# Second pair's gate and up blocks: the fifth K chunk's high-by-low products in seven-product form

## Chip, cores and metric

One core of a Trainium2 chip runs the whole kernel. The metric is device time in microseconds of one launch, the median over runs.

## The reference

```python
def _A_ref(x, wqkv, wo):                     # linear attention, 32 heads of 20
    ...
    pq, pk = phi(q), phi(k)                  # phi(t) = where(t > 0, t + 1, exp(t)) + 1e-6
    kv = jnp.einsum("bhsd,bhse->bhde", pk, v)
    ...
    return (lambda x, *d: x.transpose(*d))(o, 0, 2, 1, 3).reshape(B, S, D) @ wo

def _B_ref(x, w_gate, w_up, w_down):
    g = jnp.einsum("bsd,df->bsf", x, w_gate)
    u = jnp.einsum("bsd,df->bsf", x, w_up)
    h = _sigmoid(g) * u
    return jnp.einsum("bsf,fd->bsd", h, w_down)

g = _sigmoid((x * gate_w).sum(-1, keepdims=True))
return g * a + (1 - g) * b                   # S 2048, D 640, F 1536, all float32
```

The change concerns `x @ w_gate` and `x @ w_up` for the second half of the work.

## The kernel before

TensorE reads each float32 number as two parts, a high one (the rounded value) and a low one (the rest). A product of 128x128 weights with 128x512 of x is three matmuls in `mm3` (lines 406 to 408): high by high, high by low, low by high. `split` makes the parts: a copy on ScalarE (line 419), a difference on VectorE (line 423). `vec3` (line 427) is VectorE's (a op scalar) op b.

x has 2048 columns, in four groups of 512. The groups go in pairs, groups 2 and 3 first (`pr` = 1), then 0 and 1 (`pr` = 0, called the second pair here). K = 640 is five chunks of 128. On a pair (two column groups) and on gate and up (two weight matrices) the first four chunks are multiplied in a form with fewer products: sums of weights and sums of x, seven products of halves in place of eight. The fifth chunk is left over and multiplied plainly.

`f_phase(pr, ...)` runs F = 1536 as twelve blocks f = 0 to 11. A block (`Block`, steps `s1` to `s7`) has 18 products, so 54 matmuls, into running sums in PSUM: `ch` (s1, s3, s5, s6), `dd` (s2) and `cc` (s4, s7). ScalarE copies `ch` out between the steps, and `dd` starts from a copy of `ch` ("seed"). The weights of a block come in three forms: `W[n, 0]` the gate (tile `wg`, 640 KB), `W[n, 1]` (`wu`, 384 KB), and `W[n, 2]` the sums, nine chunks of 128 columns in two parts (`ws`, 1152 KB). The first pair makes them and stores them in DRAM; the second loads them with `load_form` through SP. `wg` and `wu` have two buffers; `ws_tile` takes turns between two. x stands in SBUF in `xf`: plain parts `a` and `b` of the two groups, and sums `t`.

The order in `f_phase` is f: s3, s4, s5; then f+1: s1; f: s6; f+1: s2; f: s7. In odd blocks from 3 on, the four parts d0 to d3 of a down pair (`down_pair`, 18 products of h with w_down) lie in between: d0 behind s3, d1 behind s4, d2 behind s5, d3 behind s1 of the next. Their weights come as one tile `wf`, loaded with `load_wf` behind s7 of the odd block before.

Which VectorE and ScalarE work goes where is settled when the program is made: the class `Order` keeps a model of the engines' times and puts pieces of work from queues between the steps (`fill`, `_stream` by due time, `need` when a step cannot go without). Among this work in the second pair are the denominators of the attention (`queue_dens`, on the tile `fac`: VectorE writes its groups from loads `pden`, stores them to `den_dram`, and reads back factors, `fac<-fac_dram`, through SP), the forms of the mixing matrix M (`queue_m`, tiles `mr` and `mt`), and the scaling and splitting of groups for the last stage. In that stage M's chunks `MHL[k, part]` (ten of 640 columns), loaded with `load_m`, are multiplied with `pq`, on top of seeds made on VectorE from `bl` and `omg`.

DMAs are issued on two queues, SP's and GpSimd's (POOL), each in order (line 363). An issue waits on its queue for what the load overwrites.

The lines of the loads of the second pair before:

```python
            if f + 2 < FC and not pr:
                for i in {2: (0,), 6: (1,), 7: (2,)}.get(s, ()):
                    load_form(("f", 0, f + 2), i)
```

Of the kernel before, what the change touches and what calls it, by code (L numbers as in the profile page):

```python
# [14 lines left out]
P = 128  # L15
# [15 lines left out]
class Order:  # L31

    def __init__(self):
        self.slack(False)
        self.pe = self.act = self.vec = 0.0
        self.items, self.lazy, self.chain, self.spare, self.soon, self.urgent = [], [], [], [], [], []
        self.kept = []
        self.made, self.used, self.done, self.before, self.tags, self.seeded = {}, {}, {}, {}, {}, {}
        self.streams, self.plan, self.base, self.turn = {}, {}, 0.0, 0
        self.busy = False  # L40
        self.parts = self.pend = None

    def slack(self, long):
# [216 lines left out]
    def mm(self, out, w, first, *aps):  # L260
        at = self.data(out if first else None, aps)
        if not first:
            p = self.place(out)
            at = max(at, self.last(self.used, p), self.seeded.get(p[0], 0.0))
        self.pe = max(self.pe, at)
        self.pe += 0.014 + w / 2400
        for ap in (*aps, out):
            self.busy_till(self.place(ap)[0], [self.pe + P_LAG])

    def when(self, ap):  # L270
        return self.last(self.made, self.place(ap))
# [98 lines left out]
def v_cost(w):  # L370
    return 0.07 + w / 960

@with_exitstack
def gated_mix_kernel(ctx: ExitStack, tc: tile.TileContext, x0, xt, xn, wk, wv, wo, wst_q, wst_f, out_t):
# [10 lines left out]
    def f32(ap):  # L385
        return ap.bitcast(F32)

    def width(ap):
        n = 1
        for s in ap.shape[1:]:  # L390
            n *= s
        return n
# [17 lines left out]
        order.mm(out, width(out), False, l_hi, r_lo)  # L410
        order.mm(out, width(out), False, l_lo, r_hi)

    def prod(out, terms, first):
        for n, t in enumerate(terms):
            mm3(out, *t, first and n == 0, n == len(terms) - 1)

    def act(out, src, fn, after="", **kw):
        order.on_act(width(out), after, out, src)
# [39 lines left out]
    fac = common.tile([P, NG, TG], F32, name="fac")  # L458
# [881 lines left out]
    class Block:  # L1340
# [53 lines left out]
        def s7(self):  # L1394
            prod(self.cc, [self.xb(2, 2 + j, 2 + j) for j in range(2)] + [self.xb(2, 4, 4)], False)
            add(self.c12, self.cc, self.c12, "p")

    spare_e = []

    def phi_q(g, u, src, after="p"):  # L1400
# [51 lines left out]

    def queue_dens(*gs2):

        st = {}

        def load(g, u):
            if u < KC:
                st[g, u] = tt("pden")
                gp.dma_start(st[g, u], p_dram[:, u, g])  # L1460
                st["at", g, u] = lambda: order.when(st[g, u])

        def one(g, u):
            td = fac[:, g]
            if u == 0:
                vec1(td, st[g, u], zcol[:, 0:1], zeps[:, 0:1], OP.mult, OP.add)
            else:
                vec3(td, st[g, u], zcol[:, u:u + 1], td, OP.mult, OP.add)
            load(g, u + 2)
            if u == KC - 1:  # L1470
                gp.dma_start(den_dram[:, g], td)
                st["at", g, u + 1] = lambda: order.when(den_dram[:, g])

        def turn_in(g):
            for j in range(4):
                js = slice(j * H, (j + 1) * H)
                gp.dma_start(fac[js, g].rearrange("h (d c) -> h d c", c=P),
                                  den_dram[:, g, j * P:(j + 1) * P].rearrange("(d h) c -> h d c", h=H))
            st[g, "gs"] = tt("gs")[:, :P]
            sp.dma_start(st[g, "gs"], gate_rep[4 * g:4 * g + 4].rearrange("i h c -> (i h) c"))  # L1480
            st["at", g, KC + 1] = lambda: max(order.when(fac[:, g]), order.when(st[g, "gs"]))

        def factor(g):
            td = fac[:, g]
            q = td[:, :P]
            add(td[:, :2 * P], td[:, :2 * P], td[:, 2 * P:])
            add(q, q, td[:, P:2 * P])
            order.on_vec(5 * P, "")
            nc.vector.reciprocal(q, q)
            vec2(q, q, st[g, "gs"], OP.mult)  # L1490
            gp.dma_start(fac_dram[:, g], q)
            st["at", g, KC + 2] = lambda: order.when(fac_dram[:, g])

        def turn_out(g):
            for d in range(4):
                sp.dma_start(fac[d * H:(d + 1) * H, g].rearrange("h (j c) -> h j c", c=P),
                                  fac_dram[:, g].rearrange("(j h) c -> h j c", h=H))
        order.add(0, 0, lambda: [load(g, u) for u in range(2) for g in gs2], chain=True)
        for u in range(KC):
            for g in gs2:  # L1500
                order.add(0, v_cost(TG), lambda g=g, u=u: one(g, u), None, lambda g=g, u=u: st["at", g, u]() + DEN_LAG, chain=True)
        for n, (v, fn) in enumerate(((0, turn_in), (2.0, factor), (0, turn_out))):
            for g in gs2:
                order.add(0, v, lambda g=g, fn=fn: fn(g), ("fac", g) if n == 2 else None,
                          lambda g=g, n=n: st["at", g, KC + n](), chain=True)
# [186 lines left out]
    WF = 2 * D + 8 * P  # L1692
    wf = []

    def load_wf(p):

        t = wf_tile()
        wf[:] = [t]
        for c0, c1 in ((D, 2 * D), (0, D), (2 * D, WF)):
            sp.dma_start(f32(t[:, :, c0:c1]), wd_dram[p][:, :, c0:c1])  # L1700

    def wf_tile():
        return down_pool[1].tile([P, 2, WF], F32R, name="wf", tag="wf")
# [480 lines left out]
    def q_phase(pr, b12, extra):  # L2184
# [8 lines left out]
        for j, (u, b) in enumerate(steps):  # L2193
            if isinstance(u, Block):
# [25 lines left out]
                if pr:  # L2220
                    if blk is A and s == 2:
                        queue_g(B.n)
                        queue_s(B.n, 0, 1)
                        queue_both(nx, 3)
                        queue_s(B.n, 1)
                    elif blk is A and s == 3:
                        queue_g(("f", pr, 0))
                    elif blk is A and s == 6:
                        load_w()
                    elif blk is A and s == 7:  # L2230
                        queue_s(("f", pr, 0))
                else:
                    n = {2: ((B, "f", 0, 0), (B, "f", 1, 0)), 6: ((A, "f", 0, 1), (B, "f", 1, 1)),
                         7: ((A, "f", 0, 2), (B, "f", 1, 2))}
# [27 lines left out]
    def f_phase(pr, q, hooks={}):  # L2262
# [14 lines left out]
        def step(f, s):  # L2277
            order.at((pr, f, s))
            n = ("f", pr, f)
            if s == 1:  # L2280
                order.need(("wg", n))
                blocks[f] = Block(n, f > 1 or f and not pr)
            else:
                order.need((nx[1], s))
            if pr and s == 7 and f + 1 < FC:
# [10 lines left out]
            if s == 3 and f == 0 and not pr:  # L2296
                for _ in q:
                    pass
                after_f(f, blk, 2)
# [30 lines left out]
        for f in range(FC):  # L2330
# [3 lines left out]
            if f in dens[pr]:  # L2334
                queue_dens(*dens[pr][f])
            if f % 2 and f > 1:
                if pr:
                    pass
                elif f == FC - 1:
                    while any(it[3] == "m" for it in order.spare) or order.pend:  # L2340
                        order.need("m")
                        order._flush()
                    load_m(0)
                down = down_pair(pr, f // 2 - 1)
            for s in (3, 4, 5):
                step(f, s)
# [127 lines left out]

    def load_m(i):

        n = (0, 3, 10)
        t = (ws_tile, wf_tile)[i]().rearrange("p a b -> p (a b)")[:, :(n[i + 1] - n[i]) * D]
        sp.dma_start(f32(t), mp_dram.rearrange("p a b c -> p (a b c)")[:, n[i] * D:n[i + 1] * D])
# [181 lines left out]
    class ABlock(Block):  # L2661
# [118 lines left out]
    pq_tiles(2)  # L2780
    queue_pq(2)
    load_p(3)
    pq_tiles(3)
    queue_scale(3)
    queue_pq(3)
# [109 lines left out]
```

## Time and profile before

| | us |
|---|---|
| median of three runs | 725.4 (724.84 to 725.54) |
| span of the profiled execution | 723.4 |
| TensorE busy | 719.2 (3412 matmuls) |
| VectorE busy | 580.2 |
| ScalarE busy | 365.7 |
| first matmul of s3 of f=1 in the second pair | at 451.06 |
| last block's s7 ends | at 643.57 |

The profile is of one execution, and its span runs from the first instruction to the last; the time of a run has what lies around the span as well, and the profiled execution's own time is not given apart from its span. Times of rows are from the span's start. In rows of instructions the engine follows start and duration; "PE" is TensorE's matmul, "PEld" its weight load, "DVE" VectorE, "ACT" ScalarE, "SPq" the SP queue. Matmuls overlap, so a record of one is longer than the distance to the next. Helpers record the operations, so many rows share a line; the tile names tell them apart.

### The profile page before, as it was taken

How to read it: one execution, taken by the hardware profiler on the slowest of the kernel's cores; microseconds unless marked ns; L12 is line 12 of the kernel's file. 1: busy time of each engine (PE TensorE's matmuls, PEld its weight loads, DVE VectorE, ACT ScalarE, POOL GpSimd, SP SyncE). 2: the span in 40 equal slices, each digit the busy share in tenths (PEclk: the TensorE clock that was granted, in tenths of full speed). 3: DMA queues.
4: the chain of work that ended last, by engine and by line, in shares of the span. 5: the costliest groups of instructions: out<-in, count | busy, mean ns of one | idle time of the engine just before them, and what ended most of it. 6: DMA issues, size and time to landing. Idle time of an engine off the chain costs nothing.

```text
span 723.4 us, 9843 instructions
## 1 busy us (share of the span) xinstructions
PE 719.2 (99%) x3412; PEld 608.4 (84%) x3412; DVE 580.2 (80%) x1008; ACT 365.7 (51%) x682; POOL 117.9 (16%) x199
## 2 busy tenths in 40 slices
PE   9999999999999999999999999999999999999998
PEld 8999999888888888888888888888888888888887
DVE  4988878987687889898988886467666878589995
ACT  5764748267656653545455862454334242325551
POOL 0311111113311211111211133013001213000100
PEclk9999999999999999999999999999999999999999
DMA  8464658698787866457688778976959595868733
GB/s 280 115 199 114 185 129 266 139 325 291 285 316 257 325 236 240 171 216 262 241 330 322 212 253 344 394 242 213 359 169 392 177 400 158 310 258 310 195 59 131
DMA packets 65129, 177.59 MB, mean 246 GB/s; under 512 B 11723, under 2 KB 25179, under 8 KB 61495
## 3 DMA queue, kind: packets, MB, share of 16 engines
q1 hardware_dynamic: 45126, 104.03, 43.0%
q0 software_dynamic: 19664, 72.70, 29.1%
q8 instruction: 27, 0.44, 0.3%
q10 hardware_dynamic: 288, 0.23, 0.1%
q14 instruction: 24, 0.19, 0.1%
HBM read 104.62 MB, written 67.33 MB: 238 GB/s over the span
## 4 chain that ended last, share of the span: by engine, by line
PE 99%; DVE 0%; ACT 0%; issue 0%
PE ch L406 11%; PE ch L408 11%; PE ch L407 11%; PE cc L406 9%; PE cc L408 9%; PE cc L407 9%; PE dd L406 7%; PE dd L408 7%; PE dd L407 7%; PE rot L408 6%; PE rot L406 6%; PE rot L407 6%; PE rot L1577 1%; PE rot L511 0%; PE ch L996 0%; PE dd L996 0%
## 5 line engine op out<-in xcount | busy, mean ns | idle before, releaser
L423 DVE TENSOR_TENSOR hf<-c,hf 128x512 fp32r<-128x512 f32 x77 | 52.5, 687 | 19.5 <-ACT hf L419 19.1
L419 ACT ACTIVATE hf<-c 128x512 fp32r<-128x512 f32 (+1 forms) x79 | 48.5, 625 | 36.8 <-DVE c L423 36.8
L419 ACT ACTIVATE c<-ch 128x512 f32<-128x512 f32 x43 | 25.7, 598 | 73.4 <-PE ch L408 67.7
L423 DVE TENSOR_TENSOR c<-cc,c 128x512 f32<-128x512 f32 x38 | 26.2, 689 | 28.2 <-PE cc L408 15.9
L406 PE MATMUL ch<-xth,ws 128*128 128x512 f32 x112 | 43.8, 391 | 0.0
L408 PE MATMUL ch<-xth,ws 128*128 128x512 f32 x112 | 43.6, 390 | 0.0
L407 PE MATMUL ch<-xtl,ws 128*128 128x512 f32 x112 | 43.6, 389 | 0.0
L423 DVE TENSOR_TENSOR tb<-rot,tb 128x512 f32<-128x512 f32 x60 | 39.1, 684 | 2.6 <-PE rot L408 2.6
L423 DVE TENSOR_TENSOR tb<-dd,tb 128x512 f32<-128x512 f32 x41 | 28.2, 688 | 11.3 <-PE dd L408 11.2
L423 DVE TENSOR_TENSOR c<-c,c 128x512 f32<-128x512 f32 x48 | 33.0, 687 | 2.6 <-ACT c L419 2.0
L419 ACT ACTIVATE c<-dd 128x512 f32<-128x512 f32 x21 | 12.6, 598 | 43.4 <-PE dd L408 43.4
L406 PE MATMUL dd<-xrh,wg 128*128 128x512 f32 x84 | 32.9, 392 | 0.0
L408 PE MATMUL dd<-xrh,wg 128*128 128x512 f32 x84 | 32.7, 389 | 0.0
L407 PE MATMUL dd<-xrl,wg 128*128 128x512 f32 x84 | 32.7, 389 | 0.0
L406 PE MATMUL cc<-xbh,ws 128*128 128x512 f32 x84 | 32.7, 389 | 0.0
L407 PE MATMUL cc<-xbl,ws 128*128 128x512 f32 x84 | 32.7, 389 | 0.0
L408 PE MATMUL cc<-xbh,ws 128*128 128x512 f32 x84 | 32.7, 389 | 0.0
L419 ACT ACTIVATE dd<-ch 128x512 f32<-128x512 f32 x22 | 12.8, 583 | 32.2 <-PE ch L408 32.2
L423 DVE TENSOR_TENSOR wst<-wst 128x256 f32<-128x256 f32 (+2 forms) x69 | 27.4, 412 | 1.4
L408 PEld LDWEIGHTS ch<-xth,ws 128*128 128x128 f32 x112 | 21.0, 188 | 4.7 <-DVE ws L423 0.3
L407 PEld LDWEIGHTS ch<-xtl,ws 128*128 128x128 f32 x112 | 21.0, 188 | 4.3
L406 PEld LDWEIGHTS ch<-xth,ws 128*128 128x128 f32 x112 | 21.0, 188 | 4.1
(710 smaller groups left out, 2347.4 us busy)
## 6 DMA issues: line engine op xcount, KB each, us to landing
wf<-ws POOLq DMA_DIRECT2D x12, 1152.0 KB, 7.6
ws<-wf SPq DMA_DIRECT2D x11, 1152.0 KB, 9.6
wst<-wst_f SPq DMA_DIRECT2D x12, 640.0 KB, 5.0
wf<-wg POOLq DMA_DIRECT2D x12, 640.0 KB, 6.8
wd<-wd POOLq DMA_DIRECT2D x12, 640.0 KB, 8.2
wg<-wf SPq DMA_DIRECT2D x12, 640.0 KB, 6.9
wf<-wd SPq DMA_DIRECT2D x10, 640.0 KB, 11.0
xnst<-xn SPq DMA_DIRECT2D x16, 320.0 KB, 3.8
```

Source lines behind the costliest of these rows:

```text
L406: nc.tensor.matmul(out, l_hi, r_hi, start=first, stop=False, skip_group_check=True)
L407: nc.tensor.matmul(out, l_hi, r_lo, start=False, stop=False, skip_group_check=True)
L408: nc.tensor.matmul(out, l_lo, r_hi, start=False, stop=last, skip_group_check=True)
L419: nc.scalar.activation(out, src, fn, **kw)
L423: nc.vector.tensor_tensor(out, a, b, op=op)
L1577: nc.tensor.matmul(ps[:w, :w], v[:, m, :w], gt[:, m, c0:c0 + w], start=(m == 0), stop=(m == KC - 1))
```

## The change

In blocks f = 1 to 11 of the second pair the fifth chunk, too, is done with shared products, but only its high-by-low and low-by-high parts: the three high-by-high products stay, and sums of low parts (with the factor `UP`, 4096, to keep parts apart) are put in places where the sums of the first four chunks already run. `EBlock` has 53 matmuls in place of 54. It needs four sums of x (`ET`, made once, at f = 0) and three 128x128 sums of weights per block (`queue_e`). The tiles for these come out of the space of the sums' second buffer: one `ws` tile holds the `ET` and the chunk "d" of two blocks, the other the pieces of the sums of one block (`EF["w"]`), so that each piece is loaded when its step in the block before is through; f = 1 takes its pieces in `fac`. The loads of `wf` and of M move.

```diff
+    def prod(out, terms, first, singles=()):
+        ...
+        for n, (w, x) in enumerate(singles):
+            nc.tensor.matmul(out, w, x, start=False, stop=n == len(singles) - 1, skip_group_check=True)
...
+    def e_pieces(f):
+        base = EF["f" if f == 1 else "w"]
+        for i, (c0, n) in enumerate(((0, 4), (4, 4), (8, 8))):
+            EW[f, i] = base[:, c0 * P:(c0 + n) * P].rearrange("p (a c) -> p a c", a=2)
+        e = EF["x"]
+        EW[f, "d"] = e[:, 12 * P:14 * P] if f % 2 else e[:, 16 * P:]
+        EW[f, "u"] = e[:, 14 * P:16 * P] if f % 2 else EF["w"][:, 16 * P:]
+
+    def load_piece(f, i):
+        src = w_dram["f", f, 2]
+        if i == "d":
+            sp.dma_start(f32(EW[f, i]).rearrange("p (a c) -> p a c", a=2), src[:, :, 4 * P:5 * P])
+        else:
+            c0, n = ((0, 2), (2, 2), (5, 4))[i]
+            sp.dma_start(f32(EW[f, i]), src[:, :, c0 * P:(c0 + n) * P])
+
+    def queue_e(f):
+        ...
+            vec3(u[:, :P], f32(dh), -1 / UP, f32(ul), OP.mult, OP.add)
+            vec3(u[:, P:], f32(ul), UP, f32(uh), OP.mult, OP.add)
+            vec3(dl, f32(dh), 1 / UP, f32(dl), OP.mult, OP.add)
+        order.add(0, 3 * v_cost(P), fn, ("e", f), lambda: max(order.when(d), order.when(WT[n, 1])),
+                  stream=("e", f), due=order.due((0, f, 3)))
+
+    def queue_et(late):
+        (ah, al), (bh, bl) = xf.a(4, every), xf.b(4, every)
+        if late:
+            def t3():
+                vec3(bl, f32(bh), 1 / UP, f32(bl), OP.mult, OP.subtract)
+        ...
+        for k, fn in ((2, lambda: sub(t[0], f32(bl), f32(al))),
+                      (2, lambda: vec3(t[1], f32(t[0]), -UP, f32(bh), OP.mult, OP.add)),
+                      (4, lambda: sub(t[2], f32(ah), f32(t[1])))):
+            order.add(0, v_cost(TG), fn, ("et", k), stream=("et", 0), due=order.due((0, 1, 3)))
+
+    class EBlock(Block):
+        ...
+        def s1(self):
+            self.ch, self.dd = ps_tile("ch"), ps_tile(self.tag)
+            gh, _, _, xl = self.xa(0, 4, 4)
+            prod(self.ch, [self.xa(0, j, j) for j in range(2)], True, [(gh, xl)])
+            act(self.dd, self.ch, AF.Copy, "p")
+        def s2(self):
+            gh, gl, xh, _ = self.xa(0, 4, 4)
+            prod(self.dd, [self.xa(0, k, k) for k in range(2, 4)], False, [(gh, xh), (gl, xh)])
+        def s3(self):
+            order.need(("et", 2), False)
+            order.need(("e", f), False)
+            prod(self.ch, self.xt(2, 0, 1), False, [(self.e("u")[0], ET[2])])
+        def s4(self):
+            prod(self.cc, self.xt(2, 7, 0), True, [(uh, xh), (self.e("u")[1], ET[1])])
+        def s5(self):
+            prod(self.ch, self.xt(2, 5, 2), False, [(self.e("d")[0], ET[3])])
+        def s6(self):
+            prod(self.ch, self.xt(1, 0, 3), False, [(uh, xh), (ul, ET[4])])
+        def s7(self):
+            prod(self.cc, [self.xb(2, 2 + j, 2 + j) for j in range(2)], False, [(w, xh) for w in self.e("d")])
...
+        nonlocal fac                       # in queue_dens
+        if "f" in EF:
+            EF.pop("f")
+            fac = fac_tile()
...
+                    if s == 7 and blk is B:            # in q_phase, ahead of f = 0
+                        EF["x"] = order.in_views(ws_tile().rearrange("p a b -> p (a b)"))
+                        EF["f"] = order.in_views(fac_tile(F32R).rearrange("p a b -> p (a b)"))
+                        e_pieces(1)
+                        for i in (0, 2, 1, "d"):
+                            load_piece(1, i)
...
+            if 1 < f < FC - 1 and not pr and s in (3, 5, 7):
+                load_piece(f + 1, {3: 0, 5: 2, 7: 1}[s])
+            if f and not f % 2 and s == 5 and not pr:
+                load_wf(f // 2 - 1, True)              # the last cut of wf
             if f + 2 < FC and not pr:
-                for i in {2: (0,), 6: (1,), 7: (2,)}.get(s, ()):
+                for i in {2 if f < 2 else 3: (0,), 6: (1,)}.get(s if f < 2 or s != 6 else 0, ()):
                     load_form(("f", 0, f + 2), i)
+                if s == 7 and f == 0:
+                    queue_et(True)
+                    EF["w"] = order.in_views(ws_tile().rearrange("p a b -> p (a b)"))
+                    e_pieces(2)
+                    for i in ("d", 0, 2, 1):
+                        load_piece(2, i)
+                    queue_e(2)
+                elif s == 7:
+                    e_pieces(f + 2)
+                    load_piece(f + 2, "d")
+                    if f > 1:
+                        load_form(("f", 0, f + 2), 1)
+                    queue_e(f + 2)
...
             for _ in down:
                 pass
+            if not pr and f % 2 and f > 1:
+                load_wf(f // 2) if f < FC - 1 else load_m(0)
...
-            if not pr and f % 2 and 1 < f < FC - 1:    # was behind step(f, 7)
-                load_wf(f // 2)
...
-        n = (0, 3, 10)                                 # load_m: chunks 0 to 2 in ws, 3 to 9 in wf
-        t = (ws_tile, wf_tile)[i]().rearrange("p a b -> p (a b)")[:, :(n[i + 1] - n[i]) * D]
+        n = (0, 7, 10)                                 # chunks 0 to 6 in wf, 7 to 9 in ws
+        t = (wf_tile, ws_tile)[i]().rearrange("p a b -> p (a b)")[:, :(n[i + 1] - n[i]) * D]
...
-        (FC - 1, 7): [lambda: load_m(1)],
...
     load_p(3)
+    load_m(1)
```

`load_m(0)` stood ahead of s3 of f = 11 before, and moves behind its down pair. `in_views` and `views` make `Order` keep account of a tile by its parts.

More of the change, by code (lines that the diff above doesn't have):

```diff
@@ L267, in mm, with in_views @@
         for ap in (*aps, out):
-            self.busy_till(self.place(ap)[0], [self.pe + P_LAG])
+            p = self.place(ap)
+            self.busy_till(p[0], [self.pe + P_LAG])
+            if p[0] in self.views:
+                self.note(self.used, p, [self.pe + P_LAG])
+    def in_views(self, ap):
+        name = self.place(ap)[0]
+        self.before[name] = None
+        self.views.add(name)
+        return ap
     def when(self, ap):
@@ L411, in mm3 @@
         order.mm(out, width(out), False, l_lo, r_hi)
-    def prod(out, terms, first):
+    def prod(out, terms, first, singles=()):
         for n, t in enumerate(terms):
-            mm3(out, *t, first and n == 0, n == len(terms) - 1)
+            mm3(out, *t, first and n == 0, n == len(terms) - 1 and not singles)
+        for n, (w, x) in enumerate(singles):
+            nc.tensor.matmul(out, w, x, start=False, stop=n == len(singles) - 1, skip_group_check=True)
+            order.mm(out, width(out), False, w, x)
     def act(out, src, fn, after="", **kw):
@@ L457, in gated_mix_kernel, with fac_tile @@
     common.tile([P, 8], F32, name="shift")
-    fac = common.tile([P, NG, TG], F32, name="fac")
+    def fac_tile(dt=F32):
+        return common.tile([P, NG, TG], dt, name="fac", tag="fac")
+    fac = fac_tile()
     p_dram = dram.tile([P, KC, NG, TG], F32, name="p_dram")
@@ new lines, in queue_e, with fn @@
+    def queue_e(f):
+        n = ("f", 0, f)
+        d, u = EW[f, "d"], EW[f, "u"]
+        dh, dl = d[:, :P], d[:, P:]
+        uh, ul = (W[n, 1][c][:, 2 * P:] for c in range(2))
+        def fn():
+            vec3(u[:, :P], f32(dh), -1 / UP, f32(ul), OP.mult, OP.add)
[3 more added lines that the diff above has]
+                  stream=("e", f), due=order.due((0, f, 3)))
@@ new lines, in queue_et @@
+    def queue_et(late):
[3 more added lines that the diff above has]
+                vec3(bl, f32(bh), 1 / UP, f32(bl), OP.mult, OP.subtract)
+            order.add(0, v_cost(TG), t3, ("et", 3), stream=("et", 3), due=order.due((0, 1, 5)))
+            ET[3] = bl
+            return
+        t = [EF["x"][:, i * TG:(i + 1) * TG] for i in range(3)]
+        ET.update({1: t[0], 2: t[1], 4: t[2]})
+        for k, fn in ((2, lambda: sub(t[0], f32(bl), f32(al))),
+                      (2, lambda: vec3(t[1], f32(t[0]), -UP, f32(bh), OP.mult, OP.add)),
+                      (4, lambda: sub(t[2], f32(ah), f32(t[1])))):
+            order.add(0, v_cost(TG), fn, ("et", k), stream=("et", 0), due=order.due((0, 1, 3)))
@@ new lines, in gated_mix_kernel, with w, e @@
+    class EBlock(Block):
+        def w(self, i, c):
+            if i < 2:
+                return super().w(i, c)
+            f = self.n[2]
+            i, c = (0, c) if c < 2 else (1, c - 2) if c < 4 else (2, c - 5)
+            t = EW[f, i][:, :, c * P:(c + 1) * P]
+            return t[:, 0], t[:, 1]
+        def e(self, k):
+            t = EW[self.n[2], k]
+            return t[:, :P], t[:, P:]
+        def s1(self):
[6 more added lines that the diff above has]
+            prod(self.dd, [self.xa(0, k, k) for k in range(2, 4)], False, [(gh, xh), (gl, xh)])
+            self.c11 = c_tile("c11")
+        def s3(self):
+            f = self.n[2]
+            order.need(("et", 2), False)
+            order.need(("e", f), False)
+            self.c12 = c_tile("c12")
+            prod(self.ch, self.xt(2, 0, 1), False, [(self.e("u")[0], ET[2])])
+            act(self.c12, self.ch, AF.Copy, "p")
+        def s4(self):
+            self.cc = ps_tile("cc")
+            uh, _, xh, _ = self.xb(1, 2, 4)
+            prod(self.cc, self.xt(2, 7, 0), True, [(uh, xh), (self.e("u")[1], ET[1])])
+        def s5(self):
+            order.need(("et", 3), False)
+            self.c22 = c_tile("c22")
+            prod(self.ch, self.xt(2, 5, 2), False, [(self.e("d")[0], ET[3])])
+            act(self.c22, self.ch, AF.Copy, "p")
+            add(self.c22, self.cc, self.c22, "a")
+        def s6(self):
+            order.need(("et", 4), False)
+            uh, ul, xh, _ = self.xa(1, 2, 4)
+            prod(self.ch, self.xt(1, 0, 3), False, [(uh, xh), (ul, ET[4])])
+        def s7(self):
+            xh = xf.b(4, every)[0]
+            prod(self.cc, [self.xb(2, 2 + j, 2 + j) for j in range(2)], False, [(w, xh) for w in self.e("d")])
+            add(self.c12, self.cc, self.c12, "p")
@@ L1453, in queue_dens @@
     def queue_dens(*gs2):
+        nonlocal fac
+        if "f" in EF:
+            EF.pop("f")
+            fac = fac_tile()
         st = {}
@@ L1693, in gated_mix_kernel, with load_wf @@
     wf = []
[L1695 to L1700, printed above, removed]
+    def load_wf(p, later=False):
+        cuts = ((D, 2 * D), (0, D), (2 * D, WF))
+        if not later:
+            wf[:] = [wf_tile()]
+        for c0, c1 in cuts[2:] if later else cuts[:2]:
+            sp.dma_start(f32(wf[0][:, :, c0:c1]), wd_dram[p][:, :, c0:c1])
     def wf_tile():
@@ L2281, in step @@
                 order.need(("wg", n))
-                blocks[f] = Block(n, f > 1 or f and not pr)
+                blocks[f] = Block(n, f > 1) if pr or not f else EBlock(n, True)
             else:
@@ L2298, in step @@
                     pass
+                queue_et(False)
+                queue_e(1)
                 after_f(f, blk, 2)
@@ L2336, in f_phase @@
             if f % 2 and f > 1:
[L2337 to L2343, printed above, removed]
                 down = down_pair(pr, f // 2 - 1)
@@ L2475, in load_m @@
     def load_m(i):
-        n = (0, 3, 10)
-        t = (ws_tile, wf_tile)[i]().rearrange("p a b -> p (a b)")[:, :(n[i + 1] - n[i]) * D]
-        sp.dma_start(f32(t), mp_dram.rearrange("p a b c -> p (a b c)")[:, n[i] * D:n[i + 1] * D])
+        while any(it[3] == "m" for it in order.spare) or order.pend:
+            order.need("m")
+            order._flush()
+        n = (0, 7, 10)
+        t = (wf_tile, ws_tile)[i]().rearrange("p a b -> p (a b)")[:, :(n[i + 1] - n[i]) * D]
+        for j0, j1 in ((0, 4), (4, 7), (7, 10))[2 * i:2 + i]:
+            sp.dma_start(f32(t[:, (j0 - n[i]) * D:(j1 - n[i]) * D]),
+                         mp_dram.rearrange("p a b c -> p (a b c)")[:, j0 * D:j1 * D])
         for j in range(n[i], n[i + 1]):
```

5 lines of the change are left out of this document (4 added, 1 removed).

## The prediction

> **What bounds the kernel now.** I read the page first: its busy line and the chain that ended last.
>
> ```profile
> span 723.4 us, 9843 instructions
> PE 719.2 (99%) x3412; PEld 608.4 (84%) x3412; DVE 580.2 (80%) x1008; ACT 365.7 (51%) x682; POOL 117.9 (16%) x199
> ...
> PE 99%; DVE 0%; ACT 0%; issue 0%
> ```
>
> TensorE is busy for 719.2 of 723.4 us, and the chain that sets the end is TensorE for 99% of the span. The waits, asked for TensorE alone, have one row, at the very start:
>
> ```profile
> PE rot L511 <- PEq L2886: 0.8, 1, 0.8
> ```
>
> So no matmul of the changed stage waits for VectorE, ScalarE or a DMA that the profile shows. Next come stretches cut at the block boundaries of the second pair's gate and up stage (us, then busy us and count of PE, PEld, DVE, ACT, POOL, then clock, DMA share, GB/s):
>
> ```profile
> 451.06:463.30 12.24, 12.24 (x55) 10.13 (x54) 4.66 (x7) 4.05 (x7) 0.00 (x0) 1.00 1.02 410
> 463.30:475.54 12.24, 12.24 (x55) 10.14 (x54) 9.45 (x15) 4.47 (x8) 2.14 (x4) 1.00 0.69 251
> 549.01:573.52 24.51, 24.51 (x109) 20.27 (x108) 19.91 (x34) 7.18 (x13) 6.03 (x11) 1.00 0.66 245
> ```
>
> Stretches of 12.24 us hold one block, 54 matmuls by their weight loads; those of 24.5 us hold a block and a down pair. TensorE is busy to the last digit in all, at clock 1.00. 12.24 / 54 = 0.2267 us per matmul: the price of one removed, as long as nothing else gets late. The bound of this stage is the number of matmuls.
>
> **The change, part by part.**
>
> Matmuls. Counting the products of `EBlock`: s1 6+1, s2 6+2, s3 6+1, s4 6+2, s5 6+1, s6 6+2, s7 6+2, together 53 against the 54 of `Block`. Blocks f=1 to 11 are changed: 11 x 0.2267 = 2.49 us less on the path. A rule of the Trainium skill gives less: the page "TensorE: Matmul & The Clock Gate", section "Back-to-back issue gap", puts a sustained stream of weight load and matmul at about 131 ns for 512 columns, by which the sum would be 11 x 0.131 = 1.44 us; the stretches above differ from it, 227 ns, so I sum by them.
>
> VectorE. Added are three 128x128 `vec3` for each of 11 blocks and four 128x512 ones at f=0. The nearest rows (busy, mean ns):
>
> ```profile
> L423 DVE TENSOR_TENSOR fac<-fac,gs 128x128 f32<-128x128 f32 x4 | 1.2, 292 | 0.1
> L427 DVE SCALAR_TENSOR_TENSOR pl<-pl,fac 128x512 f32<-128x512 f32 x3 | 2.0, 683 | 0.0
> ```
>
> 33 x 0.29 + 4 x 0.68 = 12.3 us of VectorE, 0.88 per block. Its cover is VectorE's idle time: in the fullest stretch with a down pair 24.51 - 19.91 = 4.6 us, in the fuller of the single blocks above 12.24 - 9.45 = 2.8. Each operand is due a whole block after its data was asked for, and its product comes last in its step, behind six others. I take nothing; if the cover is gone, one late operand costs at most its own group, 0.88 us, and the first four at f=0 2.7. The tightest of these is the in-place low part of `xf.b(4)`: it may start only behind s7 of f=0 and is due at the end of s5 of f=1.
>
> ```profile
> 451.06 0.39 PE L406 MATMUL ch<-xth,ws 128*128 128x512 f32 x1
> ...
> 455.82 0.39 PE L406 MATMUL ch<-xah,wg 128*128 128x512 f32 x1
> ```
>
> The first row starts s3 of f=1, right behind s7 of f=0; the second starts what follows s5. That leaves 4.5 us for 0.7, and VectorE is busy 4.66 of 12.24 in that stretch.
>
> ScalarE gets no new work, but steps of nine matmuls now have eight, so that each copy out of the running sum `ch`, or into `dd`, has 1.81 us of cover in place of 2.04. The copy behind s5 lives with six (1.36 us) today, and gets seven. ScalarE starts at once:
>
> ```profile
> 456.02 0.60 ACT L419 ACTIVATE c<-ch 128x512 f32<-128x512 f32 x1 [1.76 <-PE ch L408]
> 457.38 0.58 ACT L419 ACTIVATE dd<-ch 128x512 f32<-128x512 f32 x1 [0.76 <-PE ch L408]
> ```
>
> It stood idle before both, waiting for TensorE; 0.6 us of work under 1.81: nothing.
>
> Loads of the forms. One load of 1152 KB per block, two blocks ahead into two buffers, becomes four: pieces of 256, 512 and 256 KB into one buffer, and "d" of 128 KB, still doubled. A piece may be asked for only when its last reader is through, one block ahead. The times to landing (us, median):
>
> ```profile
> ws<-wf SPq DMA_DIRECT2D x11, 1152.0 KB, 9.6
> ...
> ws<-wf SPq DMA_DIRECT2D x3, 256.0 KB, 4.0
> ```
>
> The tightest loads are those of an even block for the next, in today's times f=2 for f=3:
>
> ```profile
> 464.66 0.39 PE L406 MATMUL cc<-xth,ws 128*128 128x512 f32 x1
> ...
> 468.06 0.39 PE L406 MATMUL ch<-xah,wg 128*128 128x512 f32 x1
> ...
> 475.54 0.39 PE L406 MATMUL ch<-xth,ws 128*128 128x512 f32 x1
> ...
> 479.63 0.39 PE L406 MATMUL cc<-xth,ws 128*128 128x512 f32 x1
> ```
>
> The 256 KB piece is free when s3 of f=2 ends (464.66) and read when s3 of f=3 starts (475.54): 10.9 us. The 512 KB piece is free when s5 ends (468.06) and read from s4 of f=3 on (479.63): 11.6 us. That of s7 has longer. For 512 KB the landing lies between the two sizes above, 4.0 to 9.6; the first is nearer by size, and I take 5. Both are covered even by the upper end, provided that SP can issue at once. Of the queue: SP issues 34 loads more, and each piece load waits on SP for TensorE, with the next gate form, "d", the up form and the rest of `wf` behind it; all of these have a block or more until they are read. The first `wf` cuts go out behind the down pair, before s6, not behind s7, the last cut at s5 of the next block; the bytes stay as they were. Nothing, if SP is free; where it isn't is the first rival.
>
> `fac` lends its space to the pieces of f=1, read up to the end of s7 at 463.30, where the second stretch begins. The denominators' first write there comes later today too, so this costs nothing:
>
> ```profile
> 464.11 0.99 DVE L434 TENSOR_SCALAR fac<-pden,zcol,zeps 128x512 f32<-128x512 f32 x2
> ```
>
> The mixing matrix. Today the first three chunks are loaded into `ws` at 630.5, eleven us ahead of the rest, and seven into `wf` at 641.7. After it, seven go into `wf` in two loads, and three (960 KB) behind `load_p(3)`, when `ws` is free. They enter a full queue:
>
> ```profile
> 630.50 0.40 SPq L363 DMA_DIRECT2D ws<-mp_dram  x1
> 641.73 0.32 SPq L363 DMA_DIRECT2D wf<-mp_dram  x1
> 642.10 1.60 SPq L363 DMA_DIRECT2D pl<-p_dram  x3
> 643.80 1.49 SPq L363 DMA_DIRECT2D bl<-b_dram  x3
> ```
> ```profile
> 646.00:648.00 2.00, 2.00 (x11) 1.65 (x10) 1.38 (x3) 2.00 (x4) 0.00 (x0) 1.00 1.01 430
> 664.00:666.00 2.00, 2.00 (x10) 1.67 (x9) 2.00 (x5) 0.00 (x0) 0.00 (x0) 1.00 0.93 359
> ```
>
> 960 KB are 983 thousand bytes; at 430 GB/s they push what is behind them back by 2.3 us. First there are the three `bl`, the sums that seed the last stage:
>
> ```profile
> bl<-b_dram SPq DMA_DIRECT2D x3, 256.0 KB, 11.8
> ...
> 657.50 1.30 DVE L423 TENSOR_TENSOR dd<-bl,omg 128x512 f32<-128x512 f32 x2
> ...
> 659.89 0.39 PE L406 MATMUL dd<-pq,wf 128*128 128x512 f32 x1
> ```
>
> They land at about 643.8 + 11.8 = 655.6, the first seed that is needed is written by about 658.2, the matmul comes at 659.9. Pushed back by 2.3 it lands at 657.9 and the seed is ready at about 658.8 (0.7 of work, 0.2 of the rest): 1.1 us are left. The cost lies between 0 and 2.3 us; by the row, nearer to 0, which I take. The three chunks themselves: 641.7 plus 2240, 1280 and 960 KB at 430 GB/s (10.7 us) is 652.4, and they are read from 661 on.
>
> Sum: 723.4 - 2.5 = 720.9 us of span. The median of the runs shown, 725.4, lies 2.0 above the span; with that kept, 722.9 us, 0.34% less. The measurement can tell 0.2%, 1.45 us.
>
> **The rivals.**
>
> One: SP stands in a wait when the single buffered piece is to be asked for, and TensorE waits for the piece (slower). The place is f=10:
>
> ```profile
> 610.81 2.14 SPq L363 DMA_DIRECT2D wf<-wd  x3
> 615.60 11.37 SPq L363 DMA_DIRECT2D fac<-fac_dram  x8
> 627.07 0.52 SPq L363 DMA_DIRECT2D wg<-wd  x1
> ```
> ```profile
> 615.01 0.39 PE L406 MATMUL ch<-xah,wg 128*128 128x512 f32 x1
> ...
> 626.57 0.39 PE L406 MATMUL cc<-xth,ws 128*128 128x512 f32 x1
> ```
>
> Eight small loads hold SP from 615.6 to 627.0; the order written out today has them behind s3 and s4 of f=10. The 512 KB piece of f=11 is asked for behind s5 of f=10, at 615.0 today, so behind the eight, and is read at 626.6. If they take as long as now, it goes out at 627, lands 4.0 to 9.6 us later, and TensorE loses 4.4 to 10 us; less the 2.5 that is 727.3 to 733, about 728. The change is undone when the piece goes out later than 626.6 + 2.5 - 5 = 624.1. Against it: most of SP's waits in that stretch are for the `wf` loads just ahead,
>
> ```profile
> SPq L363 <- DMA wf<-wd: 6.2, 3, 3.4
> SPq L363 <- DMA fac_dram<-fac: 3.9, 2, 2.5
> ```
>
> and these loads now go out some 6 us earlier, or behind the piece. Without the 6.2 us the eight are through by 620.8 and the piece lands by 625.8, 0.8 us ahead of its reader; a mild form loses a few tenths to 3 us. The Trainium skill speaks for this rival: by "DMA: Bandwidth & Descriptors", section "Anatomy of one DMA — SWDGE (gpsimd) path", a semaphore wait happens on the issuing sequencer before dispatch, so everything behind it stands too; the rows of SP agree with it.
>
> Two: the edges cost more than taken. Late seeds at 659.9 (to 2.3 us), a late operand here and there (0.88 each), ScalarE held by a fuller VectorE in the two fullest stretches. With one such edge, 0.5 to 2.3 us back: 723.4 to 725.2, about 724.2; half of this lies within 0.2% of before. For it speaks that VectorE has 2.00 of 2.00 in the last stage, against it that TensorE shows no wait at all today.
>
> Three: the pieces share a tile, and a load into one part makes the readers of another wait; then the change doesn't do what it says. Each of nine blocks would wait the 4.0 us of a piece in s4: about 36 us, 759. Against it, parts of one tile at work at once:
>
> ```profile
> 485.16 0.55 POOL L363 DMA_DIRECT2D den_dram<-fac  x1 [7.24 <-DVE fac L427]
> ...
> 487.18 0.74 DVE L427 SCALAR_TENSOR_TENSOR fac<-pden,zcol,fac 128x512 f32<-128x512 f32 x1
> ...
> den_dram<-fac POOLq DMA_DIRECT2D x2, 256.0 KB, 3.0
> ```
>
> VectorE writes one group of `fac` at 487.2 while a store, out from 485.2 to about 488.2, reads another, without a wait.
>
> Four: a removed matmul gives less than the pitch. Each is recorded with 0.39 us and starts 0.227 behind the last, so 0.16 lies beside its neighbour; if its neighbours took that much longer without it, eleven would give 11 x (0.227 - 0.16) = 0.7 us: 724.7, within 0.2%. All stretches speak against it: one price per matmul, whatever the mixture. The rule of the Trainium skill's TensorE page above goes the same way, less far: 724.0 by its figure.
>
> **How the numbers follow.** My forecast 0.60 (722.9, its own range 722.3 to 723.5, by the spread of the three runs and a late operand); two 0.19; one 0.11, and 0.04 in its mild form; three and four 0.03 each. The range runs from 722.3 to 725.2, over the forecast, two, four and most of the mild form; left out are one and three, 0.14 and a little. Faster by over 0.2%, below 723.95: 0.60 and half of two, 0.70; within: the rest of two, four and the mild form, 0.16; slower: one and three, 0.14.
>
> **What would show it.** Right: 3401 matmuls, 1045 VectorE instructions, stretches of one block of 53 x 0.2267 = 12.0 us, still without a wait of TensorE; SP issuing the 512 KB piece of f=11 by about 621; the seeds done before their matmul. Wrong: a wait of TensorE for a load into `ws` or for `bl` seeds, VectorE rows ahead of ch or cc products, or a pitch other than 0.227.

## The result and the profile after

The changed kernel takes 732.6 us (median; 732.05 to 734.18), the one before 725.3. The ratio is 1.0106, with an interval from 1.0094 to 1.0119: slower by 7 us, where 2.5 us less had been forecast. Two executions (one of lag_m below, 1871 us, one of the kernel before, 4160 us) took far longer than the rest, and the ratios and intervals leave them out. First the page of the changed kernel (span, busy line, chain that ended last), then TensorE's waits (total us, times, longest):

```profile
span 732.5 us, 9922 instructions
PE 721.5 (98%) x3401; PEld 607.3 (83%) x3401; DVE 589.2 (80%) x1045; ACT 366.1 (50%) x682; POOL 118.0 (16%) x199
...
PE 92%; DVE 3%; DMA 2%; ACT 1%; issue 1%; POOL 0%; SPq 0%; DVEq 0%; POOLq 0%; ACTq 0%
```
```profile
PE ch L418 <- DVE pq L437: 2.9, 1, 2.9
PE dd L417 <- ACT dd L433: 1.7, 2, 1.5
PE ch L417 <- ACT c L433: 1.4, 1, 1.4
```

The eleven matmuls are gone (3412 to 3401), but TensorE, which waited nowhere in the changed stage before, now has stops, and the chain runs through VectorE, ScalarE and DMAs. (Lines have moved: `mm3` is 417 to 419, single products 428, ScalarE's copy 433, VectorE's two-operand work 437, `vec3` 441, DMA issue 374.) The stretch of one block (columns as in the prediction's stretches):

```profile
451.64:463.66 12.02, 12.02 (x55) 9.95 (x53) 5.87 (x11) 4.05 (x7) 0.76 (x2) 1.00 1.04 367
```

12.02 / 53 = 0.2268 us: the price of a matmul is what it was, and eleven times that, 2.5 us, was gained in this stage. So with the span 9.1 us longer (the profiled execution is the slowest of the four, 734.18), 11.6 must be found. Distances between matmuls beyond 0.227 us sum to 4.0 us from 506 to 520 and to 6.4 from 661 to 709. Some 0.6 us is a later start of the first pair (its first matmul with `wg` came at 141.1 here and 140.5 before, and between 140.3 and 141.1 in the kernels shown here, changed or not). Of the 0.6 left, 0.35 lies behind the last matmul, and the rest is not placed.

**The stops at 506 to 520.** The timeline of VectorE, ScalarE and TensorE (start, duration; in brackets the idle time before and what ended it):

```profile
497.13 0.68 DVE L437 TENSOR_TENSOR hf<-c,hf 128x512 fp32r<-128x512 f32 x1
504.26 0.75 DVE L437 TENSOR_TENSOR fac<-fac 128x256 f32<-128x256 f32 x2 [6.45 <-DMA fac<-den_dram]
...
506.25 0.68 DVE L437 TENSOR_TENSOR c<-cc,c 128x512 f32<-128x512 f32 x1
```
```profile
506.96 0.63 ACT L433 ACTIVATE c<-c 128x512 f32<-128x512 f32 x1 [4.11 <-DVE c L437]
507.50 0.58 ACT L433 ACTIVATE c<-ch 128x512 f32<-128x512 f32 x1
```
```profile
506.30 0.39 PE L428 MATMUL ch<-xrl,wg 128*128 128x512 f32 x1
508.13 0.50 PE L417 MATMUL ch<-xth,wu 128*128 128x512 f32 x1 [1.45 <-ACT c L433]
```

VectorE stands 6.45 us at one instruction, the denominators' factor, whose data are not there. Nothing of that is needed by TensorE soon, but behind it in VectorE's order stands `c<-cc,c`, behind that ScalarE's `c<-c`, behind that on ScalarE's own queue the copy `c<-ch` that frees `ch`, and s6 starts 1.6 us late. Why the factor was late is seen on the queues that issue DMAs, POOL's and SP's:

```profile
489.26 0.55 POOL L374 DMA_DIRECT2D den_dram<-fac  x1 [4.53 <-DVE fac L441]
491.51 0.54 POOL L374 DMA_DIRECT2D mp_dram<-mt  x1 [1.71 <-DVE mt L437]
494.32 0.54 POOL L374 DMA_DIRECT2D den_dram<-fac  x1 [2.26 <-DVE fac L441]
495.05 2.21 POOL L374 DMA_DIRECT2D fac<-den_dram  x4 [0.19 <-issue]
498.29 2.17 POOL L374 DMA_DIRECT2D fac<-den_dram  x4 [1.02 <-DMA den_dram<-fac]
```
```profile
494.70 1.20 SPq L374 DMA_DIRECT2D wf<-wd  x2
```

In the kernel before, the second store went out at

```profile
488.22 0.55 POOL L363 DMA_DIRECT2D den_dram<-fac  x1 [2.51 <-DVE fac L427]
```

So VectorE's own chain to that store is 6.1 us later, and the loads that follow share the DMA engines with 2 x 640 KB of `wf` that used to go out at 500.96. The plan did move the factor: VectorE comes to it at 497.8, before at 492.96. What the plan did not allow for is how long the loads take here: the four that the factor waits for landed 5.9 to 7.7 us after their issue (2.4 to 3.5 in the kernel before), while the DMA engines were busy at 0.98 (498 to 502; 0.81 in the kernel before).

**The stops of the last stage.** SP, VectorE, TensorE, and a stretch with the granted clock (the third number from the end):

```profile
681.53 1.53 SPq L374 DMA_DIRECT2D out_t<-mt  x2
683.16 1.15 SPq L374 DMA_DIRECT2D omg<-gate_dram  x2
```
```profile
690.71 1.30 DVE L437 TENSOR_TENSOR dd<-tb,omg 128x512 f32<-128x512 f32 x2 [2.01 <-DMA omg<-gate_dram]
...
694.32 1.89 DVE L437 TENSOR_TENSOR pq<-hf,pq 128x512 fp32r<-128x512 f32 x3
```
```profile
691.82 0.39 PE L417 MATMUL ch<-pq,wf 128*128 128x512 f32 x1
695.06 0.50 PE L418 MATMUL ch<-pq,wf 128*128 128x512 f32 x1 [2.86 <-DVE pq L437]
...
696.63 0.63 PE L417 MATMUL ch<-pq,wf 128*128 128x512 f32 x1
697.06 0.63 PE L418 MATMUL ch<-pq,wf 128*128 128x512 f32 x1
```
```profile
697.00:699.00 2.00, 2.00 (x6) 1.57 (x5) 1.39 (x3) 1.50 (x3) 0.00 (x0) 0.50 0.95 143
```

In the kernel before, `out_t<-mt` and `omg` went out at 675.65 and 676.63. Here a late VectorE writes `mt` late, SP stands at its store, `omg` behind it goes out 6.5 us later (2.2 of this is that the whole stage starts later), VectorE waits 2.0 us for `omg` in front of `pq`, and TensorE waits 2.9 us for `pq`. Then it costs once more: after the stop the granted clock is 0.50, and eight matmuls come 0.43 us apart in place of 0.227, some 1.7 us with the edges of that stretch.

### The profile page after: what moved, and what is told of

The parts are those of the page before. It is cut to its first block, busy times and chain, and to the rows that moved or that the text cites. A ratio compares the mean times of both kernels' runs of the same rounds, so it can differ in the third digit from the quotient of the medians.

```text
span 732.5 us, 9922 instructions
## 1 busy us (share of the span) xinstructions
PE 721.5 (98%) x3401; PEld 607.3 (83%) x3401; DVE 589.2 (80%) x1045; ACT 366.1 (50%) x682; POOL 118.0 (16%) x199
## 4 chain that ended last, share of the span: by engine, by line
PE 92%; DVE 3%; DMA 2%; ACT 1%; issue 1%; POOL 0%; SPq 0%; DVEq 0%; POOLq 0%; ACTq 0%
PE ch L418 10%; PE ch L419 10%; PE ch L417 10%; PE cc L418 7%; PE cc L419 7%; PE cc L417 7%; PE dd L417 7%; PE dd L418 7%; PE dd L419 7%; PE rot L419 5%; PE rot L418 5%; PE rot L417 5%; PE ch L428 1%; PE cc L428 1%; DMA fac<-den_dram 1%; DMA omg<-gate_dram 1%
## 5 line engine op out<-in xcount | busy, mean ns | idle before, releaser
L417 PE MATMUL ch<-xth,ws 128*128 128x512 f32 x108 | 42.2, 391 | 0.0
L419 PE MATMUL ch<-xth,ws 128*128 128x512 f32 x108 | 42.1, 390 | 0.0
L418 PE MATMUL ch<-xtl,ws 128*128 128x512 f32 x108 | 42.1, 389 | 0.0
L417 PE MATMUL dd<-xrh,wg 128*128 128x512 f32 x73 | 28.7, 394 | 1.5 <-ACT dd L433 1.5
L418 PE MATMUL dd<-xrl,wg 128*128 128x512 f32 x73 | 28.4, 390 | 0.0
L419 PE MATMUL dd<-xrh,wg 128*128 128x512 f32 x73 | 28.4, 389 | 0.0
L417 PE MATMUL cc<-xbh,ws 128*128 128x512 f32 x71 | 27.6, 389 | 0.0
L418 PE MATMUL cc<-xbl,ws 128*128 128x512 f32 x71 | 27.6, 389 | 0.0
L419 PE MATMUL cc<-xbh,ws 128*128 128x512 f32 x71 | 27.6, 389 | 0.0
L433 ACT ACTIVATE c<-c 128x512 f32<-128x512 f32 x31 | 19.5, 628 | 10.5 <-DVE c L437 10.2
L433 ACT ACTIVATE cx<-ch 128x512 f32<-128x512 f32 x16 | 9.6, 597 | 29.1 <-PE ch L419 28.9
L419 PEld LDWEIGHTS ch<-xth,ws 128*128 128x128 f32 x108 | 20.3, 188 | 4.5 <-DVE ws L437 0.3
```

The costliest lines, as they stand in the source:

```text
L417: nc.tensor.matmul(out, l_hi, r_hi, start=first, stop=False, skip_group_check=True)
L418: nc.tensor.matmul(out, l_hi, r_lo, start=False, stop=False, skip_group_check=True)
L419: nc.tensor.matmul(out, l_lo, r_hi, start=False, stop=last, skip_group_check=True)
L433: nc.scalar.activation(out, src, fn, **kw)
```

## The experiments

Theories at the start: V, the added VectorE work (sums of weights and of x) makes its in-order queue late; L, the moved loads (`wf`, the mixing matrix) do. Against both stands P0, that fewer matmuls do not pay at all.

**before_53**: the kernel before with 53 matmuls in blocks f = 1 to 11, nothing else changed.

```diff
-            prod(self.cc, [... self.xb(2, 2 + j, 2 + j) ..., self.xb(2, 4, 4)], False)
+            ...                                   # the same without low w by high x of the fifth chunk
```


> Before, with the last of the three matmuls of the fifth chunk left out in s7 of f = 1 to 11 of the second pair (part of that product is missing): 53 matmuls a block, nothing else changed. If a removed matmul is worth its pitch, 725.3 - 2.5 = 722.8 us and a TensorE without waits. If the last stage has no room for a TensorE that comes 2.5 us earlier (VectorE is full from 654 us on), the saving is met by waits there and the time stays near 725.

723.7 us against 725.15, ratio 0.9975 (0.9965 to 0.9984). Its one new wait of TensorE:

```profile
PE dd L406 <- DMA wf<-wd: 0.9, 1, 0.9
```

The gain of matmuls is real, 1.5 us. With the stop at that wait added back (0.9 by the row, 1.2 with the restart, by the distances of the matmuls) it is 2.4 to 2.6, an estimate that fits the 2.5: with shorter blocks TensorE came to `wf` before its load had landed. P0 falls.

**before_dve**: the kernel before with 45 VectorE operations of 0.3 us (10.6 us), placed and needed as the sums are, on a tile that nobody uses.

```diff
+    def queue_x(f, n):                            # n small vec3 on bd
+        order.add(0, n * v_cost(P), fn, ("e", f), stream=("e", f), due=order.due((0, f if f else 1, 3)))
...
+                for _ in range(4): queue_x(0, 3)
+                queue_x(1, 3)
...
+            if s == 7 and not pr and f + 2 < FC: queue_x(f + 2, 3)
```


> Before, with VectorE work of the size and due times of ET and e added (33 plus 12 operations of 120x120 in place, on a mask that is no longer used); loads and products as in before. Theory V: waits as in after, about 725.3 + 5 to 10 = 730 to 735. Theory L: the idle time of VectorE takes them, 725.3 to 726.

730.7, ratio 1.0071 (1.0056 to 1.0086). 10.6 us of work on an engine that is idle a fifth of the time cost 5.5 us, in one stop and what the clock lost behind it (last section):

```profile
628.16 0.42 ACT L419 ACTIVATE mt<-mr 128x256 fp32r<-128x256 f32 x1 [6.12 <-DMA mp_dram<-mt]
...
630.12 0.50 PE L406 MATMUL dd<-hf,wf 128*128 128x512 f32 x1 [3.28 <-ACT dd L419]
```

It is another place than in the changed kernel, but the same kind: this time ScalarE stands 6.1 us at a form of M, until a store has left the tile `mt`, and the copies that TensorE needs stand behind it. The cost isn't the 10.6 us of work; the plan comes out in another order (that store goes out at 621.55, in the kernel before at 601.14), and one instruction of it stands on a DMA.

**after_54**: the changed kernel's loads, tiles and buffers, but the fifth chunk multiplied plainly: 54 matmuls, no sums (the overridden steps of `EBlock` and the calls of `queue_e`, `queue_et` are taken out).

> After, with the plain products of the fifth chunk in place of the shared ones: 54 matmuls, no sums ET and e on VectorE; all loads as in after. Theory L (the moved loads make the waits): the wait behind fac<-den_dram at about 500 us and the late seeds and pq of the last stage stay, 732.6 + 2.5 = about 735. Theory V (the added work of VectorE makes them, directly or by pushing the denominators and M's forms back): the waits go, about 725.3 to 726.

729.4, ratio 1.0055 (1.004 to 1.007). VectorE waits 2.8 us for `fac<-den_dram` and no matmul of that stage waits for it; the last stage has its stops all the same:

```profile
PE ch L417 <- ACT pq L433: 1.2, 1, 1.2
...
PE ch L417 <- DVE mt L437: 0.5, 1, 0.5
```

So the stops of the middle need the sums; those of the last stage don't. But the sums' delay of the stores is the smaller part of why the data are late. Here the stores go out at 489.0 and 489.7, and the factor's data are there only 1.6 us sooner than in the changed kernel:

```profile
489.03 1.20 POOL L374 DMA_DIRECT2D den_dram<-fac  x2 [0.72 <-DVE fac L441]
496.15 4.37 POOL L374 DMA_DIRECT2D fac<-den_dram  x8 [5.91 <-DMA den_dram<-fac]
```
```profile
502.70 0.75 DVE L437 TENSOR_TENSOR fac<-fac 128x256 f32<-128x256 f32 x2 [2.81 <-DMA fac<-den_dram]
```

With the moved loads and no sums they are late all the same: the DMA engines are busy at 0.93 to 0.98 from 486 to 494 (0.50 to 0.62 in the kernel before), and the stores take 6.5 us to land (about 3 before). VectorE has two pieces of work on M in front of the factor here and comes to it at 499.9, not at 497.8; it stands 2.8 us, and TensorE does not notice.

**after_lag**: the changed kernel, with the plan told that the factor's data come 5 us later.

```diff
-                          lambda g=g, n=n: st["at", g, KC + n](), chain=True)
+                          lambda g=g, n=n: st["at", g, KC + n]() + DEN_LAG * (n == 1), chain=True)
```


> After, with the planner's ready time of the denominators' factor 5 us later, so that VectorE comes to it when fac<-den_dram has landed. If the stop at 497.5 to 504.3 us costs what stands on TensorE there (3.0 and about 0.9 us), it gives 732.6 - 3.9 = 728.7 us, and the waits of the last stage stay. If the last stage is late because of that stop, it gives back more, down to 723.

727.55, ratio 1.0028 (1.0016 to 1.004): 5.1 us less than the changed kernel. The wait for `fac` and the stops from 506 to 520 are gone; those of the last stage stay, 3.7 us as against 3.4 in after_54. They were 6.4 in the changed kernel; here none is over 1.6, and the clock stays at 1.00, so that the 5.1 us hold a part of that stage too. The same instruction, put later in the order, costs nothing there.

**before_m**: the kernel before with only the new loads of the mixing matrix.

```diff
     def load_m(i):
-        n = (0, 3, 10)                            # three chunks, then seven
+        n = (0, 7, 10)                            # seven (two loads, behind d3 of f=11), then three
...
     load_p(3)
+    load_m(1)
```


> The kernel before with only the new loads of the mixing matrix: seven chunks into wf behind d3 of f=11, three chunks (960 KB) behind load_p(3); 54 matmuls a block, no sums. Theory L (these loads alone set the stops of the last stage): mr, bl or omg land late, VectorE is late with seeds and pq, TensorE stops for 1 to 3 us in the last 60 us: 726.3 to 728.3. Theory V (the added VectorE work makes the last stage late, the loads don't): no new wait, 725.2, the time of before.

728.2, ratio 1.0047 (1.003 to 1.0064), 3.1 us slower than before. VectorE's and TensorE's new waits:

```profile
DVE rot L423 <- DMA mr<-b_dram: 0.7, 1, 0.7
DVE dd L423 <- DMA omg<-gate_dram: 0.6, 1, 0.6
```
```profile
PE ch L406 <- ACT pq L419: 1.2, 1, 1.2
```

The loads alone make stops there (2.6 us, all behind 688), as L says, and V's share in the last stage isn't needed.

**after_wf_s7**: the changed kernel with the first two cuts of `wf` back behind s7.

```diff
-            if not pr and f % 2 and f > 1:                     # behind the down pair
-                load_wf(f // 2) if f < FC - 1 else load_m(0)
+            if not pr and f == FC - 1:
+                load_m(0)
...
             step(f, 7)
+            if not pr and f % 2 and 1 < f < FC - 1:
+                load_wf(f // 2)
```


> The changed kernel with the first two cuts of wf back behind s7. Theory C (these cuts, moved in front of the denominators' stores and loads, make fac<-den_dram land late): VectorE's wait of 6.4 us for it falls below 3, TensorE's stops at 506 to 520 fall from 4.0 to under 1.5 us, the time from 732.6 to about 729. Theory P (the plan puts the factor ahead of its data, because the added VectorE work makes the denominators' own chain late; the cuts matter little): the wait stays above 5 us and the time within 1 us of 732.6.

729.85, ratio 1.0065 (1.005 to 1.008), 2.8 us less than the changed kernel.

```profile
DVE fac L437 <- DMA fac<-den_dram: 1.2, 1, 1.2
```
```profile
PE ch L418 <- DVE pq L437: 2.6, 1, 2.6
PE ch L417 <- DMA ws<-wf: 1.0, 1, 1.0
```

The wait for the factor falls from 6.4 to 1.2 us, although the stores to `den_dram` go out only 0.7 us sooner: the `wf` cuts were in the way of the loads (C), which now land in 2.2 to 3.3 us, not 5.6 to 7.7. TensorE's stops there fall from 4.0 to 1.3 us, and these are another wait: a piece of the sums, out on SP right behind the cuts, takes 10.3 us to land (5.9 in the changed kernel), and TensorE stands for it until 512.44. The last stage keeps its stops, 5.6 us.

**lag_out** and **lag_out_m**: after_lag, then two edits in the last stage: the first outputs stored through POOL in place of SP, and the 960 KB of the mixing matrix behind the `bl` loads.

```diff
-            sp.dma_start(rows(g, self.o[j]), src)
+            (sp if self.n else gp).dma_start(rows(g, self.o[j]), src)
```
```diff
     load_p(3)
-    load_m(1)
...
     load_b(3)
+    load_m(1)
```


> The changed kernel with the factor planned 5 us later (as measured before: 727.6) and the first outputs of the last stage stored through the POOL queue, so that omg's loads don't stand behind out_t<-mt on SP. Theory O (omg held behind that store makes pq late): VectorE's wait of 1.6 us for omg goes, TensorE's stops behind 690 fall from 2 us to under 0.5, 726 or less. Theory S (VectorE is full in the last stage and late anyway): omg earlier changes nothing, 727.0 to 728.0.

> As the one before, and the 960 KB of the mixing matrix behind the bl loads in place of ahead of them. Theory L: the wait for mr and the late seeds go too, TensorE loses under 1 us in the last stage, 724 to 725. Theory S: 727 to 728. A third case: the three chunks now land late and products wait for ws, 726 to 729.

lag_out takes 724.5 (0.9993; 0.9983 to 1.0002), 3.0 us less than after_lag: with `omg` no longer behind the store, one wait of TensorE for `pq` of 0.3 us is left. lag_out_m takes 723.1, ratio 0.9972 (0.9962 to 0.9983). Its page:

```profile
span 721.7 us, 9927 instructions
PE 717.5 (99%) x3401; PEld 606.8 (84%) x3401; DVE 588.8 (82%) x1045; ACT 365.4 (51%) x682; POOL 119.4 (17%) x201
...
PE 99%; DVE 0%; ACT 0%; issue 0%
```

With 37 more VectorE instructions than before, TensorE is the chain for 99% again.

**lag_m** (and once more for its trace, **lag_m_again**): after_lag with the 960 KB behind `bl` alone, the stores on SP as they were.

> The changed kernel with the factor planned 5 us later and the 960 KB behind the bl loads, the first outputs still on SP. Theory O (omg behind out_t<-mt on SP is the larger part of the last stage's stops): VectorE still waits over 1 us for omg, TensorE stops behind 685 by 1 us or more, 726 to 727.5. Theory L (the 960 KB are the larger part): the stops go almost wholly, 723 to 724.5.

> The kernel with the factor planned later and the 960 KB behind the bl loads once more, for its trace. Theory L: TensorE without a stop over 0.5 us in the last stage, because VectorE is no longer late there, whether or not omg is waited for. Theory O: VectorE waits over 1 us for omg, as with the 960 KB ahead.

723.4, ratio 0.9973 (0.9961 to 0.9984); the second time 723.1, in one execution. L holds: the order of one load of 960 KB takes 4.1 us off after_lag. By the two traces 3.5 us of it lie in the last stage; TensorE is 1.1 us later in after_lag's trace before that stage begins. SP's queue, first of after_lag, then of lag_m_again:

```profile
643.20 0.43 SPq L374 DMA_DIRECT2D ws<-mp_dram  x1
643.66 2.78 SPq L374 DMA_DIRECT2D bl<-b_dram  x3
...
649.73 0.32 SPq L374 DMA_DIRECT2D mr<-b_dram  x1
...
676.91 0.93 SPq L374 DMA_DIRECT2D out_t<-mt  x2
678.25 1.14 SPq L374 DMA_DIRECT2D omg<-gate_dram  x2
```
```profile
641.94 1.51 SPq L374 DMA_DIRECT2D bl<-b_dram  x3
...
647.41 0.32 SPq L374 DMA_DIRECT2D mr<-b_dram  x1
648.69 0.32 SPq L374 DMA_DIRECT2D ws<-mp_dram  x1
...
673.27 0.93 SPq L374 DMA_DIRECT2D out_t<-mt  x2
674.24 1.20 SPq L374 DMA_DIRECT2D omg<-gate_dram  x2
```

With the 960 KB ahead, `mr` goes out 2.3 us later, VectorE waits for it (1.6 us in after_lag), and 27 us on the store of `mt` goes out 3.6 us later and `omg` 4.0 us later (without the 1.1 us by which all is later: 1.2, 2.5 and 2.9). Behind `bl`, neither is waited for, and the three chunks still come in time. That lag_out takes away most of the same loss is no contradiction: late `mr` and the store ahead of `omg` are links of one chain, and cutting either is enough for most of it.

**after_out_m** and **before_out**: both last-stage edits without the lag; and the store edit on the kernel before, as a control.

> The changed kernel with both edits of the last stage and the factor planned as in the change. Theory A (the stop at 506 to 520 and those of the last stage add up): TensorE stops only around 506 to 520, 4 to 5 us over the 723.1 of the three edits together, 727 to 728.5. Theory K (VectorE's late factor is what makes the last stage late, too): stops in the last stage come back, 729 or more; or the late factor is made up for, 725 or less.

> The kernel before with the first outputs of the last stage stored through POOL: a control. Theory A (the edit only takes away a wait that the changed kernel has): 724.6 to 725.6, the time of before. Rival: the edit is a gain of its own, 723 or less, and the gain measured with the three edits isn't that of the matmuls.

after_out_m takes 727.8 (1.0034; 1.002 to 1.0048), 4.7 us over lag_out_m, with the wait for `fac` back (6.9 us) and stops of 4.4 us between 505 and 520 and 0.6 at 677: the two losses add up, as A says. before_out takes 725.2 (1.0001; 0.9991 to 1.0011): the edit only removes a wait that the change had brought.

## Why the prediction was wrong

*The matmuls* were right: 0.2268 us each, 2.5 us in all. The versions almost without stops (0.2 us) take 723.1 and 723.4 us, where the prediction said 722.9 (by a run of 2.0 us more than its span; it is about 1.7 in every run with both on record, which makes 722.6): 1.7 to 2.0 us less than before, with an interval from 1.2 to 2.8; that is what the change is worth when nothing gets late. The pieces of one tile don't hold up each other's readers (three: the changed kernel's TensorE has no wait for `ws`), the removed matmul gives its whole pitch (four), and SP was not held at f=10 (one): the eight small loads went out in two groups of under 2 us, and no matmul there waits for a piece.

*VectorE, "I take nothing"*: the failed step, together with the next. It asked whether the added operands come in time for their products, and they did: no matmul waits for a sum. (Their work was also less than the 12.3 us summed from the rows: the busy time grew by 9.0.) It priced the loss of cover at "its own group, 0.88". What was late was other work. With the sums the plan comes out in another order, the factor stands in it ahead of work that TensorE needs soon and before its data are there, and the queue is in order: 4.0 us of stops, and 5.1 by after_lag. That VectorE is idle for 20% says how much work fits, not which instruction will stand. before_dve shows the same with work that nobody reads: 5.5 us.

*The `wf` cuts, "Nothing, if SP is free"*: wrong as well. The cost was not that SP stood; what the cuts took was bandwidth, from loads of 64 KB on the other queue. Moving them back gives 2.8 us (after_wf_s7), as a share of the same 5.1. The stops at 506 to 520 need both: without the sums (after_54) the data are late and TensorE doesn't stop; with the sums and the cuts back behind s7, VectorE's wait is 1.2 us and TensorE has no stop from it.

*The mixing matrix, taken as 0 out of 0 to 2.3*: the mechanism was named (960 KB pushing what is behind them), the place was not. The prediction followed `bl` to the seeds, where TensorE lost 0.45 us, and stopped there. The next load behind, `mr`, and through a saturated VectorE the store that holds `omg`, cost 3.1 us alone (before_m) and 4.1 in after_lag's setting (3.5 by the traces), above the upper end. The row for VectorE with 2.00 of 2.00 busy was quoted as speaking for rival two; it meant that a delay there is carried along to the end instead of being absorbed. Rival two allowed one edge of at most 2.3 us; there were two, which add up, one of them with the clock on top.

The Trainium skill's rule that was weighed in rival one, that a wait happens on the issuing sequencer ("DMA: Bandwidth & Descriptors", section "Anatomy of one DMA — SWDGE (gpsimd) path"), agrees with the trace at another place: SP stood at `out_t<-mt`, and `omg` behind it went out 6.5 us later.

What stays open: which of the other moved loads fill the DMA engines from 486 to 494, and whether a smaller lag than 5 us would do.

## What to carry to other kernels

Where the order on each engine is fixed ahead, added work has to be priced by the instructions it pushes past their slots: look, on every in-order queue, for the next instruction that stands on a DMA, for what is queued behind it, and by how little that DMA lands in time today. A load that is moved slows the small loads beside it, on the other queue too (up to 7.7 us to landing here, 3.3 with the `wf` cuts elsewhere); it is to be followed through everything behind it to the end, above all where an engine has no idle time to catch up in. And when a change loses time, shift the late instruction or the load before giving up the idea: two small edits here turned a loss of 7 us into a gain of 2.

## What the runs showed of the hardware

After a stop of 3.24 us between two matmuls (691.82 to 695.06) the granted clock fell to 0.50 and matmuls came 0.43 us apart for about 3 us, a loss of 1.7 us; after 3.67 us in before_dve (626.45 to 630.12) and 3.02 us in after_wf_s7 (688.32 to 691.34) the same. Two distances of 1.85 us left it at 1.00, as did one of 2.24 in after_out_m:

```profile
510.00:512.00 2.00, 0.53 (x3) 0.29 (x2) 1.91 (x4) 1.45 (x3) 0.00 (x0) 1.00 1.02 359
```

The Trainium skill ("TensorE: Matmul & The Clock Gate", section "What's actually happening") puts the fall to half clock behind an idle window of about 3.4 us; the distances here agree roughly, the shortest of the three being 0.4 under that figure. A stop of 3 us is thus priced at nearly 5, an estimate from these three: the distance and 1.7 us behind it.
